# Attention and gated feed-forward in six chunks: every transpose on TensorE, column halves in every chunk, one x buffer, new lists

## The chip, the cores and the metric

The kernel runs on one core of a Trainium2 chip. The time is device microseconds (us) of one execution, and the kernel before takes 263.46 us, the median of three runs. The core has a matrix engine (TensorE; PE in the profile), a vector engine (VectorE; DVE), a scalar engine (ScalarE; ACT), GpSimd (POOL) and SyncE (SP). Each has its own queue of instructions and works through it in order; an instruction that must wait for another engine, or for a transfer, holds up whatever stands behind it in the same queue. SP, POOL and ACT also issue DMA transfers.

## The reference

Attention over 4 batches, 8 heads, 768 positions, 64 dimensions a head; its output, seen as 3072 tokens of 512 features, goes through a gated feed-forward layer with a residual.

```python
scores = (1 / sqrt(D)) * q @ k.transpose(0, 1, 3, 2)
stream_keep = causal & (is_sink | in_win)        # 4 sinks, window of 64
mask = where(is_retrieval[head], causal, stream_keep)
a = softmax(where(mask, scores, -1e9))           # divided by (sum + 1e-9)
x = (a @ v).transpose(0, 2, 1, 3).reshape(3072, 512)

g, val = x @ w_gate, x @ w_val                   # 512 -> 1536
ffn_out = (gelu(g) * val) @ w_out                # 1536 -> 512
out = x + sigmoid(x @ w_res) * ffn_out
```

Heads 0, 2 and 6 are retrieval heads, with the whole causal triangle; the other five see 4 sinks and a window of 64. The output is float32, the operands of the matrix products are fp16 on the chip.

## The kernel before

**Chunks.** The 3072 tokens go in six chunks of 512 (`CHUNKS`), numbered 0 to 5, each of four tiles of 128 tokens, out of one or two batches. A chunk passes through attention (scores, exponentials, mask, weights times values), normalisation by the row sums into x (float32, buffer `xtok`, and fp16, `x16`), the turning of x into feature-major `xT`, the gate and value products with gelu (`gate_value`, and `fast` with fewer products by sums of blocks), and the output products with the residual gate (`output` for the first half of chunk 0, `output_fast` from there on). Chunks overlap: while TensorE does one chunk's gate and output products, the next chunk's scores and exponentials are under way.

**Tasks and lists.** The program is a graph of tasks. `G.add` puts a task on one engine, `G.flex` on one of two. `PLAN` (line 54) is a fixed list of task numbers for PE, ACT, DVE, POOL and SP, followed by the buffer that each tile takes; `schedule()` replays it and works out the waits, and the engines then run their queues in that order. Nothing is reordered on the chip. Before the first gate product, TensorE also gets fillers ("warm", line 1578): products of a blank tile that keep it busy.

**Tile shapes.** TensorE works in one of several shapes: whole 128x128 tiles, rows of 64 (scores, line 1012), quarters (scores of the sinks, line 1103), or columns of 64 (transposes of q and k, line 823; window products, line 1136), where two halves go to the two halves of the array. The products of gate, value, residual, output and attention times values have no shape of their own. Where the list of thresholds at line 1618 names them from this chunk on (`able`), they may also be issued as two column halves: line 616 issues the whole product, line 617 the halves. A task that may be both takes the shape that the array is in, if that is whole or column, and columns otherwise. In the planner's model a change of shape costs 0.1 (`SWITCH`).

**q and k to feature-major.** For chunks 0 and 1 (`ROWS_UNTIL = 2`), `loads_rows` loads q and k through POOL's queue into the staging tiles `qks` and turns them on TensorE in column halves (line 823), with a copy out of PSUM on DVE or ACT (line 835). For chunks 2 to 5, `loads_natural` loads each tile of 128 positions by two transfers on POOL (line 678) into one of three `qks` buffers, and one DMA transpose on SP (line 868) writes it to `kT` or `qT`: 32 of them.

**x to feature-major.** `to_features` transposes on TensorE (line 1225) and copies from PSUM. In chunks 3 to 5 (`c > DT_FIRST`, which is 2) one of the two groups of heads goes through `to_features_dma` instead (line 1216), a DMA transpose on SP: three of them.

**The output.** For the chunks in `ACCUM` (1 to 4), `store_x` (line 1443, SP) writes x itself to the output in one transfer, and POOL's transfer at line 1522 later adds the gated part to what is there. Where a tile of chunk 0 goes through `output`, DVE adds x (line 1568) and SP stores (line 1572); the rest of chunk 0 and the end of chunk 5 add x at line 1528 (in chunk 5 on DVE or POOL), and are stored by the transfer of line 1534 on SP or ACT.

The constants for the transposes and the masks are made at the start: `ident` by a memset and a mask on POOL (line 652, issued through line 636).

## Time and profile before

| | |
|---|---|
| median of three runs | 263.46 us (262.66 to 263.57) |
| profiled execution, its time | 263.71 us |
| its span, first to last instruction | 262.0 us |
| mean granted TensorE clock | 0.997 |
| DMA packets, bytes moved | 99988, 33.18 MB |
| mean rate of the transfers | 127 GB/s |

The rows of the page that the transposes and the stores have, as the profile gives them:

| group | count | us |
|---|---|---|
| accumulating stores, line 1522, issued on POOL | 16 | 15.7 busy, 5.3 to landing |
| loads of k, line 678, issued on POOL | 36 | 32.0 busy, 9.4 to landing |
| loads of q, line 678, issued on POOL | 36 | 31.5 busy, 9.4 to landing |
| stores of x, 1024 KB each, issued on SP | 4 | 6.2 to landing |
| DMA transposes into `kT`, line 868, issued on SP | 16 | first at 65.7, last at 178.7; 1.48 median, 3.21 longest |

Busy time counts what an engine executes, and on POOL also the issuing of its transfers; an engine's share is busy time over the span of 262.0. "To landing" is the median time from the issue of a transfer to the arrival of its last byte. Times of lines in the timeline are counted from the first instruction. The time of an execution is 1.7 longer than its span.

### The profile page before, as it was taken

The numbers are of one execution on the slowest core, as the hardware profiler recorded it, in microseconds if no ns is written. First come the engines' busy times: TensorE is split into PE (matmuls) and PEld (weight loads), VectorE is DVE, ScalarE is ACT, GpSimd is POOL, SyncE is SP. The second block draws the span as 40 slices with busy tenths as digits, with TensorE's granted clock in tenths as the row PEclk, the third lists the DMA queues.
The fourth block names the chain that finished last, engine by engine and source line by source line (L and its number), as shares of the span: only waits on it lengthen the run. The fifth ranks groups of instructions, "written<-read, shape, count | busy, mean of one in ns | idle before, by whom it ended". The sixth has DMA issues, their size and how long they took to land.

```text
span 262.0 us, 8065 instructions
## 1 busy us (share of the span) xinstructions
PE 253.2 (97%) x3415; PEld 180.2 (69%) x3415; DVE 205.6 (78%) x451; ACT 164.7 (63%) x295; POOL 105.8 (40%) x144
## 2 busy tenths in 40 slices
PE   7999999999999999999999999999999998999991
PEld 5667564568576578577568577688687687678881
DVE  2688477978878888778988778988688987678965
ACT  2787345886566976546988265993656984456510
POOL 8999319981069370470699300010100220110032
PEclk9999999999999999999999999999999999999998
DMA  6999999999999999999999993728710528320003
GB/s 80 174 195 207 194 195 205 153 162 176 168 120 227 202 143 116 155 209 122 98 133 140 124 222 78 233 26 127 193 27 0 80 30 99 45 40 3 4 20 142
DMA packets 99988, 33.18 MB, mean 127 GB/s; under 512 B 84592, under 2 KB 95088, under 8 KB 99952
## 3 DMA queue, kind: packets, MB, share of 16 engines
q0 software_dynamic: 72624, 18.88, 86.2%
q1 hardware_dynamic: 27184, 13.52, 28.3%
q8 instruction: 27, 0.44, 0.7%
q10 hardware_dynamic: 144, 0.26, 0.3%
q14 instruction: 9, 0.07, 0.1%
HBM read 29.36 MB, written 10.49 MB: 152 GB/s over the span
## 4 chain that ended last, share of the span: by engine, by line
PE 93%; DMA 2%; DVE 2%; ACT 2%; issue 1%; DVEq 0%; POOLq 0%
PE ps L616 48%; PE ps L617 31%; PE ps L1012 5%; PE ps L1136 2%; PE ps L1578 2%; PE ps L823 2%; DMA qks<-in_q_dram 2%; PE ps L1225 2%; PE ps L1103 1%; DVE otile L1518 1%; DVE hT L1390 0%; ACT L1110 0%; ACT srs L1462 0%; DVE otile L1528 0%; ACT ea L1028 0%
## 5 line engine op out<-in xcount | busy, mean ns | idle before, releaser
L1522 POOL DMA_DIRECT2D out_dram<-otile x16 | 15.7, 1048 | 85.2 <-DVE otile L1518 61.5
L678 POOL DMA_DIRECT2D qks<-in_k_dram x36 | 32.0, 941 | 21.3 <-DMA kT<-qks 11.7
L678 POOL DMA_DIRECT2D qks<-in_q_dram x36 | 31.5, 977 | 17.4 <-DMA qT<-qks 11.2
L616 PE MATMUL ps<-xT,wg 128*128 128x512 f16 (+1 forms) x172 | 37.4, 337 | 0.0
L1291 ACT ACTIVATE gact<-ps 128x512 f16<-128x512 f32 x38 | 22.1, 596 | 23.8 <-PE ps L616 16.0
L616 PE MATMUL ps<-xT,wv 128*128 128x512 f16 (+1 forms) x166 | 37.0, 337 | 0.0
L1293 DVE SCALAR_TENSOR_TENSOR hT<-gact,ps 128x512 f16<-128x512 f16 x38 | 25.8, 685 | 11.2 <-PE ps L616 5.3
L1365 DVE TENSOR_TENSOR ps<-ps,otile 128x256 f32<-128x256 f32 x60 | 24.7, 429 | 7.2 <-PE ps L616 3.5
L678 POOL DMA_DIRECT2D va<-in_v_dram x24 | 23.8, 999 | 4.0 <-PE ps L1136 4.0
L616 PEld LDWEIGHTS ps<-xT,wg 128*128 128x128 f16 x172 | 16.5, 98 | 11.7 <-DVE hT L1390 0.2
L1383 ACT ACTIVATE gact<-ps 128x512 f16<-128x512 f32 x30 | 16.4, 594 | 12.3 <-PE ps L616 7.6
L616 PEld LDWEIGHTS ps<-xT,wv 128*128 128x128 f16 x166 | 15.8, 98 | 9.5 <-DVE hT L1293 0.4
L1028 ACT ACTIVATE ea<-ps 128x1024 f16<-128x1024 f32 (+2 forms) x24 | 21.4, 920 | 0.9 <-PE ps L1012 0.8
L1390 DVE SCALAR_TENSOR_TENSOR hT<-gact,ps 128x512 f16<-128x512 f16 x30 | 19.0, 682 | 3.0 <-PE ps L616 1.9
L1462 ACT ACTIVATE srs<-ps 128x512 f32<-128x512 f32 x22 | 13.2, 598 | 10.6 <-PE ps L617 8.7
L616 PE MATMUL ps<-wo,hT 128*128 128x256 f16 (+1 forms) x114 | 19.5, 296 | 0.2 <-DVE hT L1390 0.2
L617 PE MATMUL ps<-xT,wv 128*64 128x512 f16 (+1 forms) x156 | 19.7, 344 | 0.0
L617 PE MATMUL ps<-xT,wg 128*64 128x512 f16 (+1 forms) x144 | 18.0, 344 | 0.0
L1494 DVE TENSOR_TENSOR otile<-otile,ps 128x256 f32<-128x256 f32 x33 | 13.4, 418 | 5.7 <-PE ps L617 3.1
L1012 PE MATMUL ps<-qT,kT 64*128 64x64 f16 (+4 forms) x391 | 17.0, 213 | 0.5 <-ACT ea L1028 0.5
L1203 DVE TENSOR_TENSOR xtok<-ps,rcp 128x512 f32<-128x512 f32 (+1 forms) x28 | 17.0, 610 | 0.6
L1361 ACT ACTIVATE ps<-ps 128x256 f32<-128x256 f32 x25 | 9.3, 370 | 10.5 <-PE ps L616 5.8
(175 smaller groups left out, 594.2 us busy)
## 6 DMA issues: line engine op xcount, KB each, us to landing
out_dram<-xtok SPq DMA_DIRECT2D x4, 1024.0 KB, 6.2
out_dram<-otile POOLq DMA_DIRECT2D x16, 256.0 KB, 5.3
va<-in_v_dram POOLq DMA_DIRECT2D x24, 128.0 KB, 9.9
qks<-in_q_dram POOLq DMA_DIRECT2D x32, 64.0 KB, 9.4
qks<-in_k_dram POOLq DMA_DIRECT2D x32, 64.0 KB, 9.4
wg<-in_moe_w_gate_dram POOLq DMA_DIRECT2D x3, 512.0 KB, 9.0
wv<-in_moe_w_val_dram POOLq DMA_DIRECT2D x3, 512.0 KB, 10.7
wo<-in_moe_w_out_dram POOLq DMA_DIRECT2D x4, 384.0 KB, 20.3
```

The costliest lines, as they stand in the source:

```text
L616: return e.matmul(o, lhsT=lhsT, rhs=rhs, **k)
L617: return [e.matmul(o[h:h + 64], lhsT=lhsT[:, h:h + 64], rhs=rhs, **k) for h in (0, 64)][-1]
L678: return G.add(eng, issue, lambda e: e.dma_start(out_ap(), in_ap), deps, prio, bufs=bufs, dma=cost, name=name, grp=grp)
L1012: return [e.matmul(at(scr)[:, oo:oo + w], lhsT=side(BB, qb, low, 1)[half, k0:k0 + 128], rhs=side(BB, qb, low, 0)[half, qq:qq + w], start=T ...
L1028: return e.activation(out=o, in_=i_, func=AF.Exp, scale=SM_SCALE)
L1203: t2 = G.add("dve", c_dve(2 * n * 64), lambda e: e.tensor_tensor(out=xview(), in0=avv(0, DHEAD), in1=scale(), op=ALU.mult), [t1] + xdeps, ...
L1291: ta = G.add("act", c_act(512), (lambda gb=gb, ga=ga, gw=gw: lambda e: e.activation(out=at(ga)[:, :], in_=at(gb)[:, gw], func=AF.Gelu))(), ...
L1293: th = G.add("dve", c_dve(512), (lambda vb=vb, ga=ga, f=f, vw=vw: lambda e: e.scalar_tensor_tensor(out=hv(f), in0=at(ga)[:, :], scalar=0.5 ...
L1365: return G.add("dve", c_dve(256), lambda e: e.tensor_tensor(out=at(ps)[:, o], in0=at(ps)[:, BL], in1=at(es)[:, 0:256], op=ALU.add), deps, ...
L1383: ta = G.add("act", c_act(512), (lambda x=x, ga=ga, both=both: lambda e: e.activation(out=two(at(ga)[:, :]), in_=both(x), func=AF.Gelu))() ...
L1390: th = G.add("dve", c_dve(512), (lambda x=x, f=f, ga=ga, both=both: lambda e: e.scalar_tensor_tensor(out=two(hv(f)), in0=two(at(ga)[:, :]) ...
L1522: t = G.add("pool", 1.0, (lambda ot=ot, r0=r0: lambda e: e.dma_start(out[r0:r0 + 128, :], at(ot)[:, :], accum_op=ALU.add))(), ends + [stor ...
```

## The change

The diff has these parts:

- `DT_FIRST` goes from 2 to 9. No chunk reaches `to_features_dma` any more, so all x transposes are on TensorE, and all chunks take their pairs of heads in `ORDER`.
- `loads_natural` no longer issues DMA transposes. For each two tiles of k, and of q, it adds a TensorE task of 16 half transposes into PSUM (`qkT`, column shape) and a copy of 128x1024 out of it on DVE or ACT (`qkE`).
- `ACCUM` takes chunk 0 in: its x is stored by `store_x`, and its gated part is added by transfers on POOL, in `output` as in `output_fast`.
- `qks` has four buffers instead of three, `gact` six instead of four, `xtok` one instead of two.
- The thresholds for column halves are 0 for all names, and `ff` (the products of `output`) joins them.
- In the last chunk the additions of x are on DVE only, and in both halves in two pieces of 256.
- Some constraints on order are added, and `PLAN` has new lists for every engine.

The constants of the lists (84 lines of `PLAN`) are left out of the diff below.

```diff
--- before.py
+++ after.py
@@ -37,7 +37,7 @@
 
 LATER = (1, 3, 0, 2)
 ROWS_UNTIL = 2
-DT_FIRST = 2
+DT_FIRST = 9
 DT_ALL = 9
 
 VK = ((1, 4), (3, 4), (4, 5), (4, 7))
@@ -52,86 +52,86 @@
 )
 
 PLAN = (
...
 )
 
 
@@ -264,7 +264,7 @@
 SWAP = -3000.0
 VK_AT = -18.5
 VS_DMA = 0
-ACCUM = range(1, 5)
+ACCUM = range(0, 5)
 LAT = {"pe": 0.20, "act": 0.10, "dve": 0.08, "pool": 0.12, "sp": 0.1}
 
 
@@ -583,7 +583,7 @@
     blank = sb("blank", [128, 256], FP16)
     wr = sb("wr", [128, NCB, D_MODEL], FP16)
 
-    P_st = Pool(many("qks", 3, [128, 2048], FP16))
+    P_st = Pool(many("qks", 4, [128, 2048], FP16))
     P_v = Pool(many("va", 2, [128, NT, NHEAD, DHEAD + 1], FP16))
     P_vs = Pool(many("vs", 2, [128, NT - 1, VS + 1], FP16))
     P_vk = Pool(many("vk", 2, [128, 8, DHEAD + 1], FP16))
@@ -594,7 +594,7 @@
     P_eb = Pool(many("eb", 1, [128, 2816], FP16))
     P_es = Pool(many("es", 2, [128, 1024], FP16))
     P_ek = Pool(many("ek", 1, [128, 640], FP16))
-    P_x = Pool(many("xtok", 2, [128, 4, D_MODEL], FP32))
+    P_x = Pool(many("xtok", 1, [128, 4, D_MODEL], FP32))
     P_x16 = Pool(many("x16", 2, [128, 2, 4, 128], FP16))
     P_xt = Pool(many("xT", 2, [128, NCB, 512], FP16))
     P_h = Pool(many("hT", 1, [128, NF, 4, 128], FP16))
@@ -603,7 +603,7 @@
     wt = sb("wt", [128, 3, NF // 2, 256], FP16)
     xs3 = sb("xs3", [128, 2, 256], FP16)
     gvt = {nm: sb(f"w{nm}t", [128, 3, 2, 128 * NP], FP16) for nm in "gv"}
-    P_ga = Pool(many("gact", 4, [128, 512], FP16))
+    P_ga = Pool(many("gact", 6, [128, 512], FP16))
     P_sr = Pool(many("srs", 2, [128, 512], FP32))
     P_ot = Pool(many("otile", 4, [128, D_MODEL], FP32))
     P_rc = Pool(many("rcp", 3, [128, 2, 4], FP32))
@@ -850,28 +850,45 @@
         if BB.q6 is None:
             BB.q6 = Buf(P_q6)
         loaded = []
-        for i in range(a, z):
+        for i0 in range(a, z, 2):
+            st = sts[(i0 - a) // 2]
             for j, src in ((1, k), (0, q)):
-                st = sts[(i - a) // 2]
-
-                def sv(i=i, j=j, st=st):
-                    o = (j * 2 + (i - a) % 2) * 512
+                toks = []
+
+                def sv(i, j=j, st=st):
+                    o = (j * 2 + i % 2) * 512
                     return at(st)[:, o:o + 512]
-                ds = [dma("pool", base, 0.45,
-                          (lambda sv=sv, o=o: lambda: sv().rearrange("p (o h d) -> p o h d", o=2, h=4)[:, o, :, :])(),
-                          src[b, :, i * 128:(i + 1) * 128, :].rearrange("(h o) p d -> o p h d", o=2)[o], bufs=[st],
-                          grp=("ld", b, i, j)) for o in range(2)]
-                for d in ds:
-                    d.late = 5.0
-                qb, qo = qplace[b, i]
-                to, o0 = (BB.kt, i * 128) if j else (qb, qo)
-                t = G.add("sp", 1.65, (lambda sv=sv, to=to, o0=o0: lambda e: e.dma_start(
-                    at(to)[:, :, o0:o0 + 128], sv(), transpose=True))(), ds, base, bufs=[st, to], dma=0.85, name="dT")
-                t.late = 2.5
+                for i in (i0, i0 + 1):
+                    for o in range(2):
+                        toks.append(dma("pool", base, 0.45,
+                                        (lambda sv=sv, o=o, i=i - i0: lambda: sv(i).rearrange("p (o h d) -> p o h d", o=2, h=4)[:, o, :, :])(),
+                                        src[b, :, i * 128:(i + 1) * 128, :].rearrange("(h o) p d -> o p h d", o=2)[o], bufs=[st],
+                                        grp=("ld", b, i0, j)))
+                        toks[-1].late = 5.0
+                qb, qo = qplace[b, i0]
+                to, o0 = (BB.kt, i0 * 128) if j else (qb, qo)
+                scr = Buf(P_ps, "scr")
+                pr = 1000 * c - 492
+
+                def tr(e, sv=sv, scr=scr):
+                    return [e.transpose(out=at16(scr)[64 * x:64 * x + 64, (2 * m + i) * 128:(2 * m + i + 1) * 128],
+                                        in_=sv(i)[:, 128 * m + 64 * x:128 * m + 64 * x + 64], identity=ident[:, :])
+                            for m in range(NPAIR) for i in range(2) for x in range(2)]
+                tt = G.add("pe", c_mm(128, 2) * NPAIR, tr, [t_ident] + toks, pr, bufs=[st, scr, to], name="qkT")
+                tt.mode = "col"
+
+                def ev(on, scr=scr, to=to, o0=o0):
+                    def fn(e):
+                        o = at(to)[:, :, o0:o0 + 256]
+                        i_ = at16(scr)[:, 0:1024].rearrange("c (m p) -> c m p", m=NPAIR)
+                        return e.tensor_copy(out=o, in_=i_) if on == "dve" else e.activation(out=o, in_=i_, func=AF.Copy)
+                    return fn
+                t = G.flex({"dve": (c_dve(1024), ev("dve")), "act": (c_act(1024), ev("act"))}, [tt], pr, bufs=[scr, to], name="qkE")
                 loaded.append(t)
                 for p in range(NPAIR):
-                    (BB.ktok if j else BB.qtok)[p, i] = t
-            if i == a:
+                    for i in (i0, i0 + 1):
+                        (BB.ktok if j else BB.qtok)[p, i] = t
+            if i0 == a:
                 values(b, a, z, base, False)
         qb, qo = qplace[b, a]
         w6 = (z - a) * 128
@@ -1281,8 +1298,8 @@
             tg = tv = None
             for c0 in (0, 2):
                 xd = [t for cb, t in xttoks if c0 <= cb < c0 + 2]
-                tg = G.add("pe", c_mm(512, 2), mk(wg, gb, c0, gw), xd + [wtok["g", f // 4], tg], pr, bufs=[gb, xtbuf], name=f"g{f}")
-                tv = G.add("pe", c_mm(512, 2), mk(wv, vb, c0, vw), xd + [wtok["v", f // 4], tv], pr, bufs=[vb, xtbuf], name=f"v{f}")
+                tg = G.add("pe", c_mm(512, 2), mk(wg, gb, c0, gw), xd + [wtok["g", f // 4], tg], pr, bufs=[gb, xtbuf], order=ph(c, "xT") if c > 1 else (), name=f"g{f}")
+                tv = G.add("pe", c_mm(512, 2), mk(wv, vb, c0, vw), xd + [wtok["v", f // 4], tv], pr, bufs=[vb, xtbuf], order=ph(c, "xT") if c > 1 else (), name=f"v{f}")
                 if c0 == 0 and c > 0:
                     for t in (tg, tv):
                         t.boost, t.prio = ([t_ for _, t_ in xttoks], pr), 1000 * c + 1499
@@ -1335,6 +1352,8 @@
         stok = {"S1": s1, "S2": s2, "S3": s3, "S4": s4}
         left = {"A11": lambda k: A(0, 0)[:, k], "A12": lambda k: A(0, 1)[:, k], "A22": lambda k: A(1, 1)[:, k],
                 "S1": lambda k: S(0)[:, k], "S2": lambda k: S(1)[:, k], "S3": lambda k: xs3[:, k, :], "S4": lambda k: S(2)[:, k]}
+        while len(lanes_) < LANES:
+            lanes_.append([Buf(P_ps, "lane"), []])
         for q in range(2 * NP):
             j, nm = q // 2, "gv"[q % 2]
             fa, fb, w, wt_ = FA + j, FB + j, (wg, wv)[q % 2], gvt[nm]
@@ -1435,7 +1454,7 @@
         add(w(0, 1), w(1, 1), w(0, 1), tall + [t1] + plain, 3)
         add(wt[:, 2], w(1, 0), wt[:, 1], [t2], 4)
 
-    stored = {}
+    stored, opened = {}, {}
 
     def store_x(c, xbuf, xtoks):
         n = 2 if c == len(CHUNKS) - 1 else 4
@@ -1495,6 +1514,10 @@
                          [t, k], pr, bufs=[D, ots[i]], name="plus")
         p1 = product(X, "A11", "B11", True, [])
         p5 = product(Y, "S1", "T1", True, [p1])
+        if pi and c:
+            for t in (ph(c, "fw")[-4], ph(c, "fw")[-3]):
+                t.order.append(opened[c])
+        opened[c] = ph(c, "fw")[-2]
         k1, k5 = keep(X, p1, 0, 0), keep(Y, p5, 1, 256)
         p6 = product(X, "S2", "T2", False, [k1] + (tas if end else []))
         k2 = keep(X, p6, 0, 256)
@@ -1510,7 +1533,7 @@
             b, t = segs[lt]
             r0 = b * SEQ + t * 128
             ot, sr = ots[i], srs[i]
-            parts = [(slice(256, 512), None, [c12]), (slice(0, 256), None, [c11])] if i == 0 and end else \
+            parts = [(slice(256, 512), None, [c12]), (slice(0, 256), None, [c11])] if i == 0 and c == len(CHUNKS) - 1 else \
                 [(slice(0, 512), None, [c11, c12])] if i == 0 else [(slice(256, 512), None, [c22])] + [(w, X, [p]) for w, p in zip(cuts, p4)]
             ends = []
             for w, src, deps in parts:
@@ -1524,11 +1547,11 @@
                 t.late = 3.5 if c < 4 else 2.5
                 continue
             adds = []
-            for w, deps in [(p[0], [t_]) for p, t_ in zip(parts, ends)] if end else [(slice(0, 512), ends)]:
+            for w, deps in [(p[0], [t_]) for p, t_ in zip(parts, ends)] if c == len(CHUNKS) - 1 else [(slice(0, 512), ends)]:
                 fn = (lambda ot=ot, lt=lt, w=w: lambda e: e.tensor_tensor(
                     out=at(ot)[:, w], in0=at(ot)[:, w], in1=at(xbuf)[:, lt, w], op=ALU.add))()
                 n = w.stop - w.start
-                adds.append(G.flex({e_: (f_(n), fn) for e_, f_ in (("dve", c_dve), ("pool", lambda n: 0.2 + n * 0.0021))[:2 if c > 4 else 1]},
+                adds.append(G.flex({e_: (f_(n), fn) for e_, f_ in (("dve", c_dve),)},
                                    deps + xtoks[lt], pr + (0 if c == len(CHUNKS) - 1 else 90), bufs=[ot, xbuf], name="add"))
             for w, deps in ((slice(256, 512), adds[:1]), (slice(0, 256), adds[1:])) if len(adds) > 1 else ((slice(0, 512), adds),):
                 fn = (lambda ot=ot, r0=r0, w=w: lambda e: e.dma_start(out[r0:r0 + 128, w], at(ot)[:, w]))()
@@ -1565,12 +1588,8 @@
                 t1 = G.add("dve", c_dve(n), (lambda fb=fb, sr=sr, ot=ot, w=w: lambda e: e.scalar_tensor_tensor(
                     out=at(ot)[:, w], in0=at(sr)[:, w], scalar=1.0, in1=at(fb)[:, w], op0=ALU.add, op1=ALU.mult))(),
                     [ta, prev_t], pr, bufs=[fb, sr, ot], name="gated")
-                t2 = G.add("dve", c_dve(n), (lambda ot=ot, lt=lt, w=w: lambda e: e.tensor_tensor(
-                    out=at(ot)[:, w], in0=at(ot)[:, w], in1=at(xbuf)[:, lt, w], op=ALU.add))(),
-                    [t1] + xtoks[lt], pr + (0 if c == len(CHUNKS) - 1 else 90), bufs=[ot, xbuf], name="add")
-
-                G.add("sp", 0.6, (lambda ot=ot, r0=r0, w=w: lambda e: e.dma_start(out[r0:r0 + 128, w], at(ot)[:, w]))(),
-                      [t2], pr - 3000, bufs=[ot], dma=0.75, name="out").late = 2.0 if c < 3 else 0.5
+                G.add("pool", 1.0, (lambda ot=ot, r0=r0: lambda e: e.dma_start(out[r0:r0 + 128, :], at(ot)[:, :], accum_op=ALU.add))(),
+                      [t1, stored[c]], pr - 3000, bufs=[ot], dma=1.0, name="out").late = 3.5
         return made
 
     for _ in range(180):
@@ -1615,12 +1634,30 @@
             t.swap = t.prio + SWAP
         elif t.eng == "pe":
             name = t.name.rstrip("0123456789")
-            for ns, back, c0, d in ((("res",), 2300, 2, 1.0), (("fw",), 2300, 3, 1.0), (("g", "v"), 0, 2, 1.0), (("av", "avk"), -300, 4, 1.1), (("xT",), -300, 4, 1.0)):
+            for ns, back, c0, d in ((("res",), 2300, 0, 1.0), (("fw",), 2300, 0, 1.0), (("ff",), 2300, 0, 1.0), (("g", "v"), 0, 0, 1.0), (("av", "avk"), -300, 0, 1.1), (("xT",), -300, 0, 1.0)):
                 if name in ns and t.prio >= 1000 * c0 + back:
                     t.able = {"col": d}
     for x in "".join(HINTS).split():
         n_, p_ = x.split(":")
         setattr(G.tasks[int(n_.strip("~"))], "swap" if n_[0] == "~" else "prio", float(p_))
+    made = {}
+    for t in G.tasks:
+        for b in [b for b in t.bufs if b.pool is P_ek and t.eng == "act"]:
+            for u in [u for x in t.bufs if x.pool is P_ps for u in x.users if u.eng == "pe"]:
+                if b not in u.bufs:
+                    u.bufs.append(b)
+                    b.left += 1
+                    b.users.insert(0, u)
+    for t in G.tasks:
+        for b in t.bufs:
+            row = made.setdefault(id(b.pool), [])
+            if b.pool in (P_ek, P_eb, P_ea, P_x, P_h) and b not in row:
+                row.append(b)
+    for row in made.values():
+        for b0, b1 in zip(row, row[1:]):
+            for t in b1.users:
+                if t is not b0.users[0] and b0.users[0] not in t.order:
+                    t.order.append(b0.users[0])
     G.whole_groups()
     span = G.schedule()
     G.assign_waits()
```

## The prediction

> **What bounds the kernel now.** I read the page's busy shares first, then the chain of work that ended last, then TensorE's waits, and last the timeline at single places, for the price of one operation.
>
> ```profile
> PE 253.2 (97%) x3415; PEld 180.2 (69%) x3415; DVE 205.6 (78%) x451; ACT 164.7 (63%) x295; POOL 105.8 (40%) x144
> ...
> PE 93%; DMA 2%; DVE 2%; ACT 2%; issue 1%; DVEq 0%; POOLq 0%
> ...
> PE ps L1578 <- DVE blank L650: 1.1, 1, 1.1
> PE ps L617 <- issue: 0.7, 1, 0.7
> PE ps L1012 <- ACT ea L1028: 0.5, 1, 0.5
> PE ps L1136 <- issue: 0.4, 1, 0.4
> PE ps L823 <- DMA qks<-in_q_dram: 0.4, 1, 0.4
> PE ps L616 <- DVE hT L1390: 0.2, 1, 0.2
> ```
>
> The reader is to see that TensorE is busy from the first microsecond to 256 of 262, that the last chain runs 93% through it, and that all its visible waits add up to 3.3 us, 1.5 of them before the first data. It works through a list in order. So an instruction added to the list lengthens the run by its own length, unless it lands on one of those waits or on a filler (the L1578 matmuls on a blank tile, all before 20 us). I find no transfer, and no DMA transpose, among the waits of the middle: taking transposes off the queues can gain almost nothing there.
>
> **Prices.** Timeline of TensorE at four places; columns are start, time to the end of the last one, engine, line, operation, count. Ends overlap the next start, so I take the distance between starts.
>
> ```profile
> 36.25 0.59 PE L616 MATMUL ps<-xT,wg 128*128 128x512 f16 x2
> 36.78 1.53 PE L823 MATMUL ps<-ident,qks 128*64 128x128 f16 x48
> 38.24 0.61 PE L616 MATMUL ps<-xT,wv 128*128 128x256 f16 x4
> ...
> 66.98 1.46 PE L616 MATMUL ps<-xT,wg 128*128 128x512 f16 x6
> 68.27 1.03 PE L616 MATMUL ps<-xT,wv 128*128 128x512 f16 x4
> ...
> 207.31 0.38 PE L617 MATMUL ps<-wt,wS 128*64 128x256 f16 x4
> 207.63 0.33 PE L1012 MATMUL ps<-qT,kT 64*128 64x384 f16 x1
> ...
> 222.32 0.61 PE L1225 MATMUL ps<-ident,x 128*64 128x128 f16 x16
> 222.77 0.82 PE L617 MATMUL ps<-wt,hT 128*64 128x256 f16 x12
> ```
>
> A whole 512-wide matmul costs 1.29/6 = 0.215 us. A transpose in column halves costs 0.45/16 = 0.028 us a half, where its neighbours have the same shape. A change of tile shape costs: 36.25 to 36.78 is 0.53, less two matmuls of 0.215, so 0.10; 36.78 to 38.24 is 1.46, less 48 x 0.028, so 0.12; 207.31 to 207.63 is 0.32, less four halves of 0.055 (222.77 to 223.42 is 0.65 for twelve), so 0.10. I take 0.11, ends 0.10 and 0.12.
>
> **The change, part by part**, counted along the compiled programs of both kernels.
>
> *Transposes of q and k.* The 32 DMA transposes of L868 become 16 groups of 16 half transposes, 256 halves: 256 x 0.028 = +7.2 us on TensorE. Lower end the same, upper end 0.030 (1.46/48 at 36.78, its changes of shape included), 7.8. Below nothing is excluded, since no wait of the middle is on a transfer. *x.* The three DMA transposes (L1216) go; the x transposes rise from 32 halves and 56 whole ones to 176 and 8. A whole one costs what two halves do, 0.056, so 24 more: +1.3. *Column halves elsewhere.* Gate, value, residual and output matmuls of chunks 0 to 3 become pairs. A pair of 256-wide halves costs 2 x 0.054 (twelve in 0.65), the whole one 0.110 (three in 0.33, 64.37 to 64.70 in the timeline): nothing. The 205 whole 65-wide ones of attention become pairs; halves run at 0.57/36 = 0.016 (177.85 to 178.42), whole ones at 0.13/4 = 0.032 (21.98 to 22.11): nothing, at most 205 x 0.002 = 0.4. *Changes of shape.* Fillers aside there are 107 in the list before and 77 after, because full-size stretches vanish: 30 x 0.11 = -3.3, ends -3.0 and -3.6. Net on TensorE: 7.2 + 1.3 - 3.3 = +5.2.
>
> [...]
>
> *Evictions.* Each group adds a copy of 128x1024 out of PSUM: 14 on ACT at 1.03 (L835, 2.1/2), two on DVE at 1.22 (L835, 2.4/2). ACT further gets five table loads at 1.28 (L1110, 6.4/5), because exponentials are now listed inside gate stages, and four more xT copies of 0.59, and loses eight copies of 0.38 and one of 0.63: about 164.7 + 19.5 = 184 of some 267, 69%. DVE gains about 7 (the two copies, eight small copies of 0.42, two xT copies): 79%. I cost these at nothing as work, covered by TensorE, but not as waits:
>
> ```profile
> 64.00:105.00 41.00, 40.48 (x443) 27.95 (x441) 34.53 (x74) 28.70 (x51) 18.84 (x24) 1.00 1.74 163
> ```
>
> In this stretch (busy times of PE, PEld, DVE, ACT, POOL) ACT has 28.7 of 41. Six of the sixteen groups fall in its successor: + 6.2 copies + 2.6 tables + 1.2, near 39 of 44, with DVE at 35. Two in-order engines at 80 to 90% beside a full one will make it wait now and then; scores need the copies, and everything queued on TensorE stands behind them. Bounds: the middle's waits of today vanish, -1.8; or ACT's excess of two such stretches shows in part, +5. I take +0.5, near the lower end, since today's stretch at 70 to 84% cost 0.5 (L1012 on ACT ea).
>
> *Loads.* PE transposes wait for q and k loads, with all of TensorE's list behind them. Today the first DMA transpose issues at 57.12; the first new group stands at about 58. Cover is nil for a late load: 9.4 us from issue to landing (page, part 6). The 1024 KB store of chunk 0's x is new and early (6.2 us to landing), competing with w_out and w_res. That is the rival below. On POOL four accumulating stores of 1.05 are added and stand, waiting for chunk 0's output, ahead of chunk 3's loads; those are needed some 35 us later, which hides it. SP loses 35 transposes and five stores, nothing of it on the path. One x buffer: the next chunk's normalisation waits for the x store; a gate stage of 20.9 us (chain) lies between. More staging, gact and lists: no instruction.
>
> *Head.* The identity's mask (L636, 0.34) now issues on POOL between the first two loads, so the second lands 0.34 later; TensorE's group at 7.11 had just waited 0.21 for that load. +0.3, lower end 0.
>
> *Tail.* Columns as before:
>
> ```profile
> 255.64 0.82 PE L617 MATMUL ps<-wt,hT 128*64 128x256 f16 x12
> 256.46 1.38 POOL L1528 TENSOR_TENSOR otile<-otile,xtok 128x512 f32<-128x512 f32 x1 [0.63 <-DVE otile L1518]
> 256.64 1.48 DVE L1518 SCALAR_TENSOR_TENSOR otile<-srs,otile 128x256 f32<-128x256 f32 x1
> 258.04 0.41 DVE L1518 SCALAR_TENSOR_TENSOR otile<-srs,ps 128x256 f32<-128x256 f32 x1
> 258.48 0.69 DVE L1528 TENSOR_TENSOR otile<-otile,xtok 128x512 f32<-128x512 f32 x1
> ```
>
> Beside POOL's addition a DVE step of 0.42 (the group's other calls) took 1.48, and a 256 KB store on ACT's queue lands 2.1 after issue, a 128 KB one on SP's 1.7 (page, part 6). After the change all eight additions are 256 wide on DVE: that step is 1.06 shorter, the last addition 0.28 (0.69 less about 0.41), the store 0.4: -1.7; the additions now all stand in DVE's queue, and one more of 0.4 can come ahead of the last: +0.4. I take -1.3, ends -2.1 and 0.
>
> **Sum.** 5.2 + 0.5 + 0.3 - 1.3 = +4.7 on the span of 262.0, so 266.7. The profiled run took 263.71, 1.7 around its span; its time is 0.25 above the median of the three, 263.46. Predicted median: 263.46 + 4.7 = 268.2.
>
> **Rivals.**
> 1. *ACT becomes a second bound* in the two stretches with six groups. For it: 39 of 44, extra tables between gelus. Against: today's waits are tiny. Price +4 more: 272.2. Chance 0.15.
> 2. *Chunk 0's x store delays w_out and w_res.* Issued on POOL at 20.7 to 24.5, they land 20 to 21 later (page, part 6), about 41 to 45; their first matmuls are at 44.8 and 46.6, so slack is about 2. The page's DMA row stands at 9 until about 155 us, and a megabyte at the 174 to 207 GB/s of its row there takes 5 to 6, if it goes ahead. Price 3 to 4 beyond slack, 271.7. Chance 0.10.
> 3. *The freed queues shorten the head* (the other side): loads land earlier, transposes replace fillers, TensorE's list starts its dense part sooner. It would have to beat +4.7 by the 1.3 that is 0.5%, so it decides only if the first gate matmul moves from 20.24 to before 14.2; time 262. Against: no DMA transpose runs before 57 us, both programs hold 63 fillers, and the first loads stand in the same order. Chance 0.04.
> 4. *It nets out*: switches at 0.12, tail -2.1, waits of the middle gone (-1.8): 8.5 - 3.6 - 3.9 = +1.0, 264.5. Chance 0.06 for ending within 0.5%.
>
> **Numbers.** My forecast has 0.65 (266 to 271). 0.5% is 1.3 us, about what a measurement here can tell from none. Slower 0.90 = 0.65 + 0.15 + 0.10; same 0.06; faster 0.04. Range: the low end is 5.2 with switches at 0.12 (-0.3), the tail at -2.1 and waits at -1.0, +1.8, so 265.2; the high end holds rivals 1 and 2: 272.5.
>
> **What would show it.** TensorE still above 95%; L874's 256 halves at 28 ns from start to start; about 77 changes of shape; offset from the list growing by few waits; span's end about 4.4 us, not 5.7 (262.0 less 255.64 + 0.65), behind the end of TensorE's list. Waits of TensorE on ACT copies in the stretches of chunks 2 and 3 beyond 3 us would show rival 1; waits of L616/L617 on DMA wo or wr near 45 us rival 2; a first gate matmul before 15 us rival 3. I am wrong if transposes lengthen TensorE's list by much less than 8.5 us.

## The result and the profile after

The kernel after takes 275.27 us (median of three, 274.74 to 276.79) against 263.46: slower by 4.7%, ratio 1.047, 95% interval 1.040 to 1.054. The forecast was 268.2 with a range up to 272.5; the direction was right, the size was not, by 7.1 us.

The page of the kernel after, busy times, the queue that brings instructions (packets, MB, share), and the chain that ended last:

```profile
PE 261.7 (96%) x4774; PEld 200.3 (73%) x4774; DVE 209.5 (77%) x470; ACT 182.5 (67%) x306; POOL 105.6 (39%) x144
...
q8 instruction: 37, 0.61, 0.9%
...
PE 75%; DMA 10%; POOL 5%; DVE 2%; ACT 2%; issue 1%; DVEq 0%
```

The chain is the first thing to see. It went 93% through TensorE before; now 15% of it are POOL's issues and one transfer: the first 53 us hang on a load of w_out. The second is the instruction queue: 37 packets of 16 KB, where the page of the kernel before has 27:

```profile
q8 instruction: 27, 0.44, 0.7%
```

TensorE's waits in the kernel after (total, times, longest):

```profile
PE ps L617 <- issue: 1.2, 3, 0.6
PE ps L617 <- DMA wo<-in_moe_w_out_dram: 1.2, 1, 1.2
PE ps L823 <- DMA qks<-in_k_dram: 1.1, 1, 1.1
PE ps L1029 <- ACT es L1045: 1.1, 2, 0.9
PE ps L1597 <- DVE blank L650: 1.1, 1, 1.1
PE ps L1029 <- ACT gact L1402: 0.8, 1, 0.8
PE ps L617 <- DVE otile L1513: 0.5, 1, 0.5
PE ps L617 <- DVE ea L1081: 0.4, 1, 0.4
PE ps L617 <- DVE ps L1384: 0.2, 1, 0.2
```

Together 7.6, against 3.3 before. The page counts a matmul's pipeline as busy, so each wait is really longer: the timeline of TensorE at the w_out load has 12 products of 0.108 a half from 50.36, which end their turn near 51.6, and the next start is 53.09, 1.5 later, of which 1.24 is shown as idle:

```profile
50.36 1.49 PE L617 MATMUL ps<-wo,hT 128*64 128x512 f16 x12
53.09 0.84 PE L617 MATMUL ps<-wo,hT 128*64 128x512 f16 x6 [1.24 <-DMA wo<-in_moe_w_out_dram]
```

Measured between starts in this way, the waits above 0.28 sum to 10.4 in this trace and to 3.3 in that of before, sums that are good to about half a us: +7.1. The difference of the spans, 273.5 - 262.0 = 11.5, then divides so:

| part | forecast | measured |
|---|---|---|
| TensorE's list itself (what is left of 11.5) | +5.2 | +6.3 |
| head, and waits in the list | +0.8 | +7.1 |
| tail behind TensorE's list | -1.3 | -1.9 |

Of the 7.1, 4.2 lie before 65 us: 0.7 more at the first load of k, 1.5 at w_out (53.09), 2.1 in three waits marked issue (23.5, 30.2 and 63.1), each of which ends 1.2 to 1.5 after a packet of the instruction queue has arrived (at 22.30, 28.71 and 61.66). The rest stands near 91 (1.8), 140 (1.1), 182 (1.2) and in the tail (0.8), less what the kernel before had in its own middle.

A trace is one execution, and the early waits differ between executions. The first load of k, issued at 2.59, landed at 8.34 here, and between 6.90 and 7.79 in the eight other traces below that issue it at the same time, so the 0.7 at the head is mostly this execution's own. The waits near 91, 140 and 182 stand in every trace of the new lists, the same to a tenth of a us, except where experiments 11 and 12 moved them.

The tail of the kernel after:

```profile
269.02 0.84 PE L617 MATMUL ps<-wt,hT 128*64 128x256 f16 x12 [0.51 <-DVE otile L1513]
...
270.02 0.41 DVE L1541 SCALAR_TENSOR_TENSOR otile<-srs,ps 128x256 f32<-128x256 f32 x1
270.13 0.34 ACTq L1557 DMA_DIRECT2D out_dram<-otile  x1
270.46 0.42 DVE L1551 TENSOR_TENSOR otile<-otile,xtok 128x256 f32<-128x256 f32 x1
```

TensorE's list ends near 269.7 (269.02 and twelve halves of 0.055) and the span at 273.5: 3.8 behind it, where it was 5.7.

### The profile page after: what moved, and what is told of

Its sections match the earlier page's. It is cut to its first block, busy times and chain, and to the rows that moved or that the text cites. A ratio compares the mean times of both kernels' runs of the same rounds, so it can differ in the third digit from the quotient of the medians.

```text
span 273.5 us, 10733 instructions
## 1 busy us (share of the span) xinstructions
PE 261.7 (96%) x4774; PEld 200.3 (73%) x4774; DVE 209.5 (77%) x470; ACT 182.5 (67%) x306; POOL 105.6 (39%) x144
## 4 chain that ended last, share of the span: by engine, by line
PE 75%; DMA 10%; POOL 5%; DVE 2%; ACT 2%; issue 1%; DVEq 0%
PE ps L617 65%; DMA wo<-in_moe_w_out_dram 10%; PE ps L1029 4%; PE ps L874 3%; PE ps L1242 2%; POOL va L678 2%; PE ps L1153 1%; POOL qks L678 1%; POOL wv L678 1%; POOL wg L678 1%; ACT es L1045 1%; DVE ps L1384 1%; PE ps L1120 1%; POOL wo L678 1%; POOL vk L738 1%
## 5 line engine op out<-in xcount | busy, mean ns | idle before, releaser
L617 PE MATMUL ps<-xT,wg 128*64 128x512 f16 (+1 forms) x488 | 60.3, 339 | 0.3 <-issue 0.3
L617 PE MATMUL ps<-xT,wv 128*64 128x512 f16 (+1 forms) x488 | 59.3, 339 | 0.0
L1545 POOL DMA_DIRECT2D out_dram<-otile x18 | 17.1, 982 | 108.3 <-DVE otile L1541 65.6
L617 PE MATMUL ps<-wo,hT 128*64 128x256 f16 (+1 forms) x444 | 35.3, 285 | 1.2 <-DMA wo<-in_moe_w_out_dram 1.2
L617 PEld LDWEIGHTS ps<-xT,wg 128*64 128x64 f16 x488 | 28.3, 110 | 10.6 <-issue 1.3
L617 PEld LDWEIGHTS ps<-xT,wv 128*64 128x64 f16 x488 | 29.0, 110 | 9.7 <-ACT gact L1402 0.3
L678 POOL DMA_DIRECT2D va<-in_v_dram x24 | 27.9, 1217 | 0.0
L617 PEld LDWEIGHTS ps<-wo,hT 128*64 128x64 f16 x444 | 22.4, 110 | 6.0 <-DMA wo<-in_moe_w_out_dram 2.1
L617 PE MATMUL ps<-wr,xT 128*64 128x512 f16 x192 | 24.2, 380 | 0.0
L1380 ACT ACTIVATE ps<-ps 128x256 f32<-128x256 f32 x23 | 8.5, 368 | 14.6 <-PE ps L617 14.2
L1029 PEld LDWEIGHTS ps<-qT,kT 64*128 64x128 f16 x391 | 9.9, 94 | 10.4 <-issue 5.5
```

Of the source, the lines that this page charges most:

```text
L617: return [e.matmul(o[h:h + 64], lhsT=lhsT[:, h:h + 64], rhs=rhs, **k) for h in (0, 64)][-1]
L678: return G.add(eng, issue, lambda e: e.dma_start(out_ap(), in_ap), deps, prio, bufs=bufs, dma=cost, name=name, grp=grp)
L1029: return [e.matmul(at(scr)[:, oo:oo + w], lhsT=side(BB, qb, low, 1)[half, k0:k0 + 128], rhs=side(BB, qb, low, 0)[half, qq:qq + w], start=T ...
L1545: t = G.add("pool", 1.0, (lambda ot=ot, r0=r0: lambda e: e.dma_start(out[r0:r0 + 128, :], at(ot)[:, :], accum_op=ALU.add))(), ends + [stor ...
```

## The experiments

Each time is a median, beside a ratio to the kernel before measured on the same chip; the kernel after has 1.047 (1.040 to 1.054), so times alone do not show a difference from it of less than about 2 us.

**1. Halves in all chunks, in the kernel before.** Only the thresholds:

```diff
-(("res",), 2300, 2, ...), (("fw",), 2300, 3, ...), (("g", "v"), 0, 2, ...), (("av", "avk"), -300, 4, ...), (("xT",), -300, 4, ...)
+(("res",), 2300, 0, ...), ..., (("ff",), 2300, 0, ...), (("g", "v"), 0, 0, ...), (("av", "avk"), -300, 0, ...), (("xT",), -300, 0, ...)
```

> The kernel before, with the thresholds of the column halves at 0 for all names and ff added; nothing else, its own lists. Matmuls 3415 to 4472, changes of shape (fillers aside) 107 to 78. Theory (a pair of halves costs what the whole product costs, and the miss of the forecast lies in waits that the new lists bring): 29 changes fewer at 0.11, little given back by the 65-wide pairs, so some 2 below the kernel before: 261.5, range 260.5 to 263.0. Rival (halves cost by themselves, by their weight loads or by the longer stream of instructions): 265 or more.

Measured: 269.74, 1.0252 (1.0191 to 1.0314). The rival's side. TensorE's waits in its trace say where:

```profile
PE ps L617 <- issue: 5.3, 3, 2.6
PE ps L617 <- DMA xT<-x: 1.6, 1, 1.6
```

"Issue" means that no semaphore held the engine. Two of its three waits end within bursts of 65-wide pairs (at 62.93 and 107.95), the third 6 us behind one (at 71.16), and each ends 1.3 to 1.5 after a packet of the instruction queue has arrived (one packet has arrived at 61.42, the matmul behind it starts at 62.93). So TensorE runs out of instructions there. Two more costs are in this trace. The granted clock is 0.51 for the 3.1 us behind the first wait, which costs 1.5. And the wait of 1.6 is for a DMA transpose of x, which the kernel after does not have: it took 9.8 to land here, 8.9 in experiment 13 and 6.6 in the kernel before.

**2. The thresholds of before, in the kernel after.** The reverse edit.

> The kernel after, with the thresholds of the kernel before, its own new lists. Matmuls 4774 to 3807, changes of shape 77 to 129. Theory (halves are free, changes cost 0.11): +5 on the kernel after, 280, range 278 to 282. Rival (halves cost by themselves): below 276, as 967 instructions fewer outweigh 52 changes.

Measured: 276.17, 1.0518 (1.0481 to 1.0554), between the two sides. 52 more changes of shape should have cost 5 to 6; the medians differ by 0.9, which the intervals do not tell from nothing. All of TensorE's waits in its trace:

```profile
PE ps L1029 <- ACT es L1045: 1.2, 2, 0.9
PE ps L1597 <- DVE blank L650: 1.1, 1, 1.1
PE ps L1029 <- DVE hT L1409: 0.8, 1, 0.8
PE ps L617 <- DVE otile L1513: 0.5, 1, 0.5
PE ps L616 <- DVE ea L1081: 0.4, 1, 0.4
PE ps L616 <- DVE ps L1384: 0.2, 1, 0.2
```

The waits marked issue and the one for w_out before 65 us are gone, and by the distance between starts the waits sum to about 5.8 instead of 10.4. In the new lists, too, most of what the halves save in changes of shape is given back in waits. The third piece of w_out lands at 49.22 here and between 51.0 and 53.1 in the five traces with the same loads, the same store and all products in halves; TensorE starts the products ahead of it at the same time (50.22, and 50.36 in the kernel after). Why it lands earlier no run shows.

**3. The supply of instructions by itself.**

```python
def pair(e, n):
    return [e.matmul(ps[h:h + 64, 0:n], lhsT=a[:, h:h + 64], rhs=b[:, 0:n], start=True, stop=True) for h in (0, 64)][-1]
```

> Not the kernel: TensorE alone on one tile, with stretches of 768 whole 65-wide products, 768 pairs of 65-wide halves, the same pairs with 48 loads of q and k and six 1 MB stores running, and the whole ones again, with 512-wide products between. Nothing of the reference is computed. Theory formed from the first four runs (TensorE's instructions come in pieces of 256, a pair of 65-wide halves uses four instructions in 0.032, so a piece lasts 2 us, less than a late piece takes to come): whole ones 768 x 0.030 = 23 to 25 us with no wait; pairs alone 25 us and up, with waits marked issue of 0.3 and more, spaced by about 128 halves; with the transfers running longer still, 30 to 45. Rival (halves are slow by themselves, by their weight loads): the pairs take evenly longer, with no waits, alone and beside the transfers alike.

Busy times of its four stretches (stretch, length, then PE, PEld, DVE, POOL, granted clock, DMA share, GB/s), in the order whole, pairs, pairs beside transfers, whole:

```profile
27.20:50.60 23.40, 23.40 (x770) 23.39 (x769) 0.00 (x0) 0.00 (x0) 1.00 0.01 4
63.50:104.70 41.20, 26.59 (x1538) 25.27 (x1537) 0.00 (x0) 0.00 (x0) 1.00 0.02 4
117.70:169.20 51.50, 30.41 (x1537) 29.05 (x1536) 0.00 (x0) 23.07 (x32) 0.90 1.07 111
182.80:206.30 23.50, 23.50 (x770) 23.34 (x767) 0.00 (x0) 0.00 (x0) 1.00 0.02 4
```

768 whole products take 23.4, 0.030 each, with no wait; the same work in pairs takes 41.2, 0.054 each, and 51.5 beside transfers (with the granted clock at 0.90, a part of it). The timeline shows the pattern:

```profile
67.92 2.22 PE L39 MATMUL ps<-b,a 128*64 128x65 f16 x128 [1.13 <-issue]
71.37 2.22 PE L39 MATMUL ps<-b,a 128*64 128x65 f16 x128 [1.24 <-issue]
```

Exactly 128 halves, then a wait, every 3.45 us, in three places 3.7 to 4.0. A half is two instructions (its weight load and its product), so a piece is 256 instructions, and TensorE uses it up in 2.04. The pages agree: the kernel after has 9548 matmuls and weight loads to 37 packets of the instruction queue, 258 a packet, the kernel before 6830 to 27, 253. With nothing else running a piece takes 3.45 to come round, 1.4 of it as a wait; beside the transfers the waits between starts reach 4.7, in a stretch that moves 312 GB/s.

**4. Which widths starve.** The same with wider halves.

> TensorE alone on one tile again: 512 pairs of 128-wide halves and 384 pairs of 256-wide ones, first alone, then with 96 loads of q and k and six 1 MB stores running. Nothing of the reference is computed. Theory (a piece of 256 instructions takes about 3.45 to come round, as in the stretch of 65-wide pairs): 128-wide pairs, which use a piece in 3.6, run at 0.028 a half with little or no wait alone, and wait beside the transfers; 256-wide pairs, a piece in 7.0, do not wait in either. Rival (any column halves wait): waits in all four stretches.

128-wide alone, 256-wide alone, then both beside transfers:

```profile
27.30:56.00 28.70, 28.70 (x1026) 28.61 (x1026) 0.00 (x0) 0.00 (x0) 1.00 0.02 4
56.00:97.90 41.90, 41.90 (x774) 41.82 (x769) 0.00 (x0) 0.00 (x0) 1.00 0.01 3
111.00:150.90 39.90, 31.43 (x1025) 30.50 (x1026) 0.00 (x0) 28.45 (x40) 0.96 1.52 149
150.90:192.80 41.90, 41.90 (x776) 41.86 (x770) 0.00 (x0) 30.23 (x41) 1.00 1.08 70
```

As expected. 128-wide halves (the width of the new transposes) use 256 instructions in 3.6, just slower than the refill: no wait alone, 8.5 of 39.9 idle beside transfers. 256-wide ones wait in neither stretch; the transfers beside them moved 70 GB/s, half of the 149 beside the 128-wide ones, so a denser load was not tried.

**5. All halves but the 65-wide ones, in the kernel before.**

```diff
-(("res",), 2300, 2, ...), (("fw",), 2300, 3, ...), (("g", "v"), 0, 2, ...), (("av", "avk"), -300, 4, ...), (("xT",), -300, 4, ...)
+(("res",), 2300, 0, ...), ..., (("ff",), 2300, 0, ...), (("g", "v"), 0, 0, ...), (("av", "avk"), -300, 4, ...), (("xT",), -300, 0, ...)
...
+                    if name not in ("av", "avk"):
+                        t.mode = "col"
```

> The kernel before, with gate, value, residual, output products and x transposes always in column halves, but the 65-wide products of chunks 0 to 3 whole; its own lists. Matmuls 3415 to 4270, changes of shape 107 to 141. Theory (only the 65-wide pairs starve TensorE of instructions; wider halves are free and a change of shape costs 0.11): +3.5 on the kernel before, ratio 1.013, range 1.009 to 1.018. Rival (any halves starve it, as 855 more matmuls are nearly the 1057 of the kernel with all in halves, which took +6.9 where its changes of shape alone would give -3): ratio 1.035 or more.

Measured: 269.45, 1.0256 (1.0230 to 1.0283), between the two. One wait marked issue is left, in a 65-wide burst of chunk 4 where the kernel before has 0.7:

```profile
PE ps L617 <- issue: 1.4, 1, 1.4
```

So in this trace wider halves don't starve TensorE in the early chunks, though they fill it there. But 34 changes at 0.11 and 0.7 of wait make 4.4 of the measured 6.7; 2.3 stay open.

**6. Three loads moved forward, in the kernel after.** In POOL's list only: 202 (w_val) ahead of 252 (q); 208 and 209 (w_out) ahead of 244 (v).

> The kernel after, with three loads moved in POOL's list alone: two pieces of w_out ahead of three loads of v, one piece of w_val ahead of a load of q, as in the kernel before. Theory (the order of the loads in the new list makes TensorE wait 1.2 to 1.5 for w_out at 53 and about 0.6 for w_val at 30): 273.3, range 272.6 to 274.2. Rival (the new 1 MB store of chunk 0's x holds up w_out, whatever the order): 275.

Measured: 278.58, 1.0602 (1.0538 to 1.0667): slower by 3.3 (the two intervals just meet), which neither side expected. The wait for w_out is gone, and so is the one at 30.18 that the theory put down to w_val (a piece of it lands at 30.01 in the kernel after, but the wait is marked issue there); this one has come:

```profile
PE ps L1154 <- issue: 5.4, 1, 5.4
```

The profiled execution is the longest of four, 280.23 at a mean clock of 0.984; two of the others took 276.8 and 277.5 at 0.993 and 0.994, so the wait is not this long in every one. The packet of instructions that ends it arrived at 61.2, while the transfers moved 160 GB/s. Busy times of PE, PEld, DVE, ACT, POOL and the granted clock around it:

```profile
50.00:57.20 7.20, 7.20 (x118) 4.26 (x114) 6.05 (x12) 5.24 (x9) 3.41 (x5) 1.00 2.32 159
57.20:62.70 5.50, 0.07 (x6) 0.04 (x3) 1.33 (x3) 0.54 (x1) 0.23 (x1) 0.89 2.26 164
62.70:70.00 7.30, 7.30 (x144) 6.39 (x146) 3.11 (x6) 2.42 (x5) 0.00 (x0) 0.62 1.06 91
70.00:80.00 10.00, 10.00 (x208) 7.85 (x206) 7.09 (x17) 7.22 (x11) 7.86 (x10) 1.00 0.95 79
```

After the wait TensorE runs 7.3 us at 0.62 of its clock, which costs 2.8 more; from 70 us on it is at 1.00 again.

**7. The same with chunk 0's store cut.**

```diff
-            out[r0:r0 + n * 128, :].rearrange("(i p) d -> p i d", p=128), at(xbuf)[:, 0:n, :]),
+            out[r0:r0 + (n if c else 1) * 128, :].rearrange("(i p) d -> p i d", p=128), at(xbuf)[:, 0:n if c else 1, :]),
```

> The kernel with the three loads moved (278.6), and chunk 0's store of x cut to one tile of four, 256 KB (the rest of chunk 0's output is then without x). Theory (the wait of 5.4 near 62 is for a piece of instructions that stood behind the transfers of that stretch, the 1 MB store among them): the wait falls below 2, 274.0, range 272.5 to 275.5. Rival (it is the loads of q and k alone, or not the transfers at all): 277.5 or more.

Measured: 275.03, 1.0469 (1.0445 to 1.0492), 3.5 less, and no wait marked issue above 0.5. So here the long wait went with the store; but with the same cut in experiment 8 the wait for instructions grows, so that they stand behind the store in particular is not shown. The time is still not below the kernel after: waits of 1.8 for q and of 1.5 for v came instead. In this stretch moving a load only chooses who waits.

**8. Only the store cut**, the same edit in the kernel after.

> The kernel after, with chunk 0's store of x cut to one tile of four, 256 KB instead of 1 MB (the rest of chunk 0's output is then without x); its own lists. Theory (up to 65 us the transfers are the bound, and the store, which the forecast priced at nothing, holds up w_out and the pieces of instructions): the waits at 53 (1.5) and 63 (0.9) shrink by more than half, 273.6, range 272.8 to 274.6. Rival (only the order of the loads counts, the store is hidden): 275 to 276.

Measured: 273.12, 1.0378 (1.0349 to 1.0408): 2.2 below the kernel after, as expected, though its interval overlaps that of the kernel after. The wait for w_out is gone (its third piece lands at 47.9, where it landed at 53.05, and between 51.0 and 52.0 in four other traces with the whole store); that near 62 grew instead of shrinking:

```profile
PE ps L617 <- issue: 2.5, 2, 2.1
```

Between starts it is 2.3 instead of 0.85, so of the 1.5 that w_out gave nothing is left. What else the two traces differ by is the wait at the head (1.3 in the kernel after, none here), and there the store, issued at 42.17, cannot reach. The store does delay w_out; that it costs 2.2 is not shown.

**9. A quarter of the new transposes.**

```diff
-                            for m in range(NPAIR) for i in range(2) for x in range(2)]
+                            for m in range(1) for i in range(2) for x in range(2)]
...
-                        i_ = at16(scr)[:, 0:1024].rearrange("c (m p) -> c m p", m=NPAIR)
+                        i_ = at16(scr)[:, 0:256].rearrange("c (m p) -> c m p", m=1).to_broadcast([128, NPAIR, 256])
```

> The kernel after, with 4 of the 16 half transposes of each of the 16 groups (the copies out of PSUM keep their size and spread one quarter; q and k of chunks 2 to 5 are then partly wrong). 192 halves fewer. Theory (they cost their length, 0.028 each): -5.4, 269.9, range 269.0 to 270.8. Rival 1 (they also starve the stream of instructions, as near 63): 268.5 or less. Rival 2 (part of them stands in waits that are there anyway): 271.5 or more.

Measured: 271.40, 1.0316 (1.0278 to 1.0354), 3.9 less than the kernel after, where 5.4 was expected; with an interval of some 1.9 on the kernel after, the difference between the two is not shown. Two of TensorE's waits in its trace:

```profile
PE ps L617 <- DMA wo<-in_moe_w_out_dram: 2.5, 2, 1.8
PE ps L1242 <- issue: 1.2, 1, 1.2
```

The first, 2.5 where the kernel after has 1.2, ends at 51.8 and 54.5, ahead of the first of these transposes (61.4), so it is not their doing; the trace of experiment 10, with all of them, has 2.4 there. The second is new (at 69.75): behind 61 us the waits marked issue come to 2.0 instead of 0.6, so fewer transposes did not mean fewer waits for instructions.

**10. The copies cut to a sixteenth.**

```diff
...
-                        o = at(to)[:, :, o0:o0 + 256]
-                        i_ = at16(scr)[:, 0:1024].rearrange("c (m p) -> c m p", m=NPAIR)
+                        o = at(to)[:, :, o0:o0 + 16]
+                        i_ = at16(scr)[:, 0:1024].rearrange("c (m p) -> c m p", m=NPAIR)[:, :, 0:16]
```

> The kernel after, with the 16 copies of 128x1024 cut to 128x64 (most of q and k of chunks 2 to 5 is then left out; two memsets on DVE at the start are added). ACT loses some 14 x 0.7, DVE 2 x 0.8. Theory (the waits of TensorE near 91, 140 and 182 come from where the new lists put scores and exponentials, not from the load of ACT): 274.8, range 274.0 to 275.8. Rival (ACT is late because of the copies, the second bound of the forecast): 273.2 or less.

Measured: 275.46, 1.0480 (1.0449 to 1.0511): no difference. ACT is 10.8 less busy than in the kernel after, and TensorE's waits for ACT and DVE in the middle are the same to a tenth:

```profile
PE ps L1029 <- ACT es L1045: 1.1, 2, 0.9
...
PE ps L1029 <- ACT gact L1402: 0.8, 1, 0.8
...
PE ps L617 <- DVE ea L1081: 0.4, 1, 0.4
```

**11. No table loads**: `AF.Gelu` and `AF.Tanh` replaced by `AF.Exp`.

> The kernel after, with gelu and tanh replaced by exponentials (the gate and the residual gate are then not the reference's), so that ACT loads one table instead of 17; same instructions and lists otherwise. Theory (the new lists put exponentials between gelus, and TensorE's waits near 91, 140 and 182 stand behind those table loads of 1.28): 3 less than the kernel after, 272.3, range 271.0 to 273.6. Rival (the copies out of PSUM that ACT got, 14 of 1.03, or the work on DVE make these waits): 274.5 to 275.5.

Measured: 274.30, 1.0449 (1.0414 to 1.0483): 1.0 less, inside the interval of the kernel after. One of the three places moved, that near 182. ACT es has 1.1 in two waits in the kernel after, 0.9 of it there; left is the one near 140:

```profile
PE ps L1029 <- ACT es L1045: 0.2, 1, 0.2
```

**12. Other products into the wait near 140**: in TensorE's list 1088 goes ahead of 1163, 1089 ahead of 1152.

> The kernel after, with two groups of output products of 6 in TensorE's list moved a little forward, into the two waits for ACT and DVE near 140 (0.64 and 0.42). Theory (these waits come from where the new list puts scores and products, and other work is at hand to fill them): -1.0, 274.3, range 273.8 to 274.9. Rival (ACT or DVE is the bound there, so that the wait moves to the next product): 275.0 or more.

Measured: 276.85, 1.0525 (1.0490 to 1.0561), slower by 1.6, with intervals that overlap: the rival's side. The products need tanh, which stands in ACT's queue behind the exponentials, so one longer wait took the place of two:

```profile
PE ps L618 <- ACT srs L1482: 1.9, 1, 1.9
```

and the clock fell again behind it (same columns as above):

```profile
139.50:141.50 2.00, 0.17 (x12) 0.04 (x4) 1.46 (x3) 2.00 (x4) 0.00 (x0) 1.00 0.00 0
141.50:147.00 5.50, 5.47 (x123) 4.58 (x125) 3.58 (x9) 2.45 (x5) 0.00 (x0) 0.69 0.01 3
```

**13. The tail alone, in the kernel before.** Four additions go from POOL's list to DVE's.

```diff
-                adds.append(G.flex({e_: (f_(n), fn) for e_, f_ in (("dve", c_dve), ("pool", lambda n: 0.2 + n * 0.0021))[:2 if c > 4 else 1]},
+                adds.append(G.flex({e_: (f_(n), fn) for e_, f_ in (("dve", c_dve),)},
```

> The kernel before, with the four additions of the last chunk that POOL made put on DVE, in unchanged sizes; the rest of its lists as it was. Theory (beside POOL's addition a step of 0.42 on DVE takes 1.48, so the tail is 1.06 shorter and DVE has room for three small additions): -0.9 on the kernel before, ratio 0.9966, range 0.994 to 0.999. Rival (the additions now stand ahead of the last steps on DVE): 1.000 or more.

Measured: 261.87, 0.9969 (0.9951 to 0.9988). The step that took 1.48 beside POOL is back to 0.42:

```profile
255.15 1.36 DVE L1528 TENSOR_TENSOR otile<-otile,xtok 128x256 f32<-128x256 f32 x3
...
256.43 0.42 DVE L1518 SCALAR_TENSOR_TENSOR otile<-srs,otile 128x256 f32<-128x256 f32 x1
```

The interval lies below 1: this version is 0.3% faster than the kernel before, and so faster than both. Its trace has no wait marked issue, where the kernel before, with the same list for TensorE, has 0.7 and 0.4: such waits come and go between executions.

**14. That, with the 65-wide products whole everywhere** (`("av", "avk"), -300, 4` becomes `-300, 9`).

> The kernel before, with the additions of the last chunk on DVE and the 65-wide products whole in all chunks. Matmuls 3415 to 2834, changes of shape 107 to 122. Theory (the two waits marked issue, 0.7 and 0.4 on the page, 1.6 by the distance between starts, go, 15 changes at 0.11 come): 0 to -0.4 on the kernel with the tail alone, ratio to the kernel before 0.996, range 0.993 to 0.999. Rival (whole products cost their changes and the waits move elsewhere): 1.001 or more.

Measured: 263.44, 1.0029 (1.0012 to 1.0047), the rival's number, but not its reason. No wait marked issue is left, and none was there to win in the trace of experiment 13 either. What remains are 15 changes of shape, 1.65 at 0.11, and the step from 0.9969 to 1.0029 is 1.6 us.

## Why the prediction was wrong, step by step

The part of the sum for TensorE's list itself, +5.2, came out at +6.3, and the tail came out nearly right. What the sum had for waits, +0.8, came out at +7.1.

- **Transposes of q and k, +7.2: the length was right.** 32 halves take 0.89 from 70.75 in the kernel after, 0.028 each. Without 192 of the 256 the time is 3.9 less (experiment 9), which the noise does not tell from their length, 5.4.
- **Changes of shape, -3.3: right as length.** With 52 of them put back (experiment 2) TensorE's list ends 0.9 later with some 4.6 less of waits, so they are worth about 5.5, 0.11 each.
- **Column halves elsewhere, "nothing": this is the step that failed.** The prediction took the price of a pair from short bursts (36 halves at 0.016) and never asked what feeds them. 65-wide pairs use a piece of instructions in 2.04, and it takes 3.45 to come: 0.054 a pair in a long stretch against 0.030 whole (experiment 3). In the lists of before all halves cost 6.9 where a gain of some 2 was expected, part of it in waits for instructions (experiment 1). In the new lists the waits before 65 us, some 3.5 without the head, are gone from the trace with the thresholds of before, and the gain of the halves shrinks from 5 or 6 to 0.9 (experiment 2). Waits marked issue are 2.1 of these; how halves make w_out late is not shown.
- **Loads, "nothing" but for rival 2 at 0.10: failed too.** The slack of 2 us was read from the kernel before; the new list issues the last two pieces of w_out behind three loads of v, at 25.78 instead of 22.98, and they land 8 us later, so TensorE waits 1.5. The order of before brings the third piece back to 45.2 (experiment 6), leaving out most of chunk 0's store to 47.9 (experiment 8); in both a wait for instructions came instead. The new order of POOL's loads could have been read beforehand.
- **Evictions as work, nothing: right** (experiment 10). **As waits, +0.5 "near the lower end": too small.** Near 91, 140 and 182 the waits sum to 4.1, where the middle of before had 1.1 outside its waits marked issue: +3.0. Rival 1 was wrong in its cause: shorter copies change none of them, and without table loads only that near 182 goes. Whole products and other loads leave them as they are too, which points to the order of the new lists; that is argued, not shown. Near 140 the moved products waited for tanh in ACT's queue (experiment 12); for 91, where scores start as a gelu on ACT ends, no other order was tried.
- **Head, +0.3: measured +0.7, which is mostly chance.** The load is issued 0.29 later, as forecast, but in eight other traces it lands at 6.90 to 7.79, against 7.03 in the kernel before.
- **Tail, -1.3: right in mechanism.** Measured -1.9 behind TensorE's list, of which the additions on DVE alone give about 0.8 (experiment 13). But TensorE now waits 0.8 for DVE ahead of its last products, where it did not before; both together are -1.1.
- **Rival 3** (an earlier dense start) did not happen: the first gate product starts at 20.94, not before 14.2. **Rival 4** (it nets out) needed the waits of the middle to go; they grew.

What stays open: 2.3 us of experiment 5, and how the early waits divide between the order of the loads, the store and the halves. Experiments 2, 6, 7 and 8 show that each moves them, and that they don't add.

## What to carry to other kernels

When an edit splits instructions, price the stream as well as the array: here TensorE was fed 256 instructions in about 3.5 us at best, so a long stretch of 65-wide halves starved it, 128-wide ones did so beside transfers, and 256-wide ones in neither stretch that was tried. In a stretch where the profile's DMA row stands at 9, don't take a new transfer as free because its own consumer has slack: here, under the new order of loads, the third piece of w_out landed at 47.9 without most of chunk 0's store, and at 49 to 53 with it. And when new order lists come with a change, read the loads' order in them before trusting slack that was measured under the old ones.

## What the runs showed of the hardware

- A wait for instructions lasted about 1.4 us with idle queues (experiment 3), and up to 4.7 there and 5.4 in a kernel (experiment 6) beside transfers.
- A wait of 5.4 on TensorE was followed by 7.3 us at a clock of 0.62, and one of 1.9 by 5.5 us at 0.69; one of 2.1 (experiment 8) was followed by none below 1.00. Why the clock fell behind a wait of 1.9 and not behind one of 2.1, no run shows.
- A change of tile shape cost about 0.11 us in whole kernels too: 15 more of them came with 1.6 (experiment 14), 52 with about 5.5 in TensorE's list (experiment 2).
